# Attention and a swish layer on one core: one laid-down order for whole chunks, and other PSUM banks for the second third of the numerators

## The chip, the cores and the metric

The kernel runs on one core of a Trainium2 chip. The metric is device time in microseconds, the median of several runs. The span of a profile, from its first to its last instruction, is a little shorter than the device time of the same run (283.0 against 284.75 us for the kernel before).

The engines have these short names: PE is TensorE, the matrix engine; DVE is VectorE; ACT is ScalarE; POOL is GpSimd; SP issues most transfers. Each has its own queue of instructions, taken in order. Matmul results go to PSUM, which has eight banks of 512 float32 columns; everything else lies in SBUF.

## The reference

An attention with a kernel in place of the softmax (relu times a cosine and a sine of the position), for 8 batches of 8 heads with 576 positions of 64 values, feeds a two-layer network with a swish between.

```python
def phi(x, c, s):
    r = np.maximum(x, 0.0)
    return np.concatenate([r * c, r * s], axis=-1)
q_p, k_p = phi(q, cos_w, sin_w), phi(k, cos_w, sin_w)
kv  = np.einsum('bhsf,bhsd->bhfd', k_p, v)
z   = np.sum(k_p, axis=2)
num = np.einsum('bhsf,bhfd->bhsd', q_p, kv)
den = np.einsum('bhsf,bhf->bhs', q_p, z)[..., None] + 1e-06
x   = (num / den)          # then rearranged to 4608 tokens of 512
h   = x @ w_in             # 512 -> 2048
g   = h * (1.0 / (1.0 + np.exp(-beta * h)))
out = g @ w_out            # 2048 -> 512
```

## The kernel before

The 4608 tokens are worked in nine chunks of 512 (c = 0 to 8). In the steady state the loop of chunk c does three things: the hidden layer of chunk c, the attention of batch b = c + 1, whose tokens are needed from the next chunk on, and the output layer of chunk c. From chunk 3 on, half of the hidden layer and all of the output layer use a scheme with seven products of half-sized blocks in place of eight. It needs sums of inputs made in advance, and additions on the results.

The names matter, because the order of the work is written down as strings of them:

- `X Y Z V` are four groups of the hidden layer in the seven-product scheme; `X1` to `X7` are the products, `c1X c5X cuX` the copies of partial results, `a2X a3X a7X` the additions, `SaX SbX` the two Silus at the end. `p0` to `p7` are the other eight groups of the hidden layer, plain ones, and `sp0` to `sp7` their Silus on ACT.
- `K` is the matmul of keys and values, `kt` takes it from PSUM; `N0 N1 N2` are the three thirds of the numerators, `x0 x1 x2` divide them (DVE) and turn them by transfers on SP.
- `s01` to `s34` are sums of the hidden values (DVE) for the output layer: the first digit is the quarter, the second the kind.
- `ox1` to `ox7`, and in the new string `oy1` to `oy7`, are the products of the two halves of the output layer.

The parts that the change touches; cuts are marked.

```python
def h_silu(c, jt, bank):                         # sp..., Sa., Sb.: on ACT
    nc.scalar.activation(gs[c, jt // 4][:, jt % 4], ps[:, bank], AF.Silu, scale=beta[:, jt : jt + 1])

def q_tan(b, jp, behind=None):                   # on POOL: q turned, times the tangent
    got = tan_mul(nc.gpsimd, qs_of(b)[:, jp], qts[b % 2][:, jp], 0, NQ)
    # behind: POOL is made to wait for the last sum
# x_rden, x_mul on DVE: den = num's last column + eps; rden = 1/den; xs = num * rden, all from PSUM

def num_all(b, t, bank):                         # a third of the numerators
    for i in range(3):
        for jp in range(2):
            num_mm(b, 3 * t + i, jp, bank, 2 * i + jp)   # to banks bank and bank + 1

# ... the output layer of one half:
def o_fast(c, pr, banks, cols=0):
    b_ps, e_ps, a_ps = (ps[:, k_, 0:HM] for k_ in banks)
    # ...
    def m1():
        prod(b_ps, g_part(0, 0), B11, True, False, 0 < cols)
        nc.scalar.copy(p1, b_ps)
    def m5():
        prod(e_ps, s_part(S1), T1, True, False, 1 < cols)
        nc.scalar.copy(p5, e_ps)
    def m6():
        prod(b_ps, s_part(S2), T2, False, False, 2 < cols)
        nc.scalar.copy(u, b_ps)
    def m2():
        prod(a_ps, g_part(1, 0), B21, True, True, 3 < cols)
    def m7():
        prod(b_ps, s_part(S3), T3, False, False, 4 < cols)
    def m3():
        prod(e_ps, s_part(S4), B22, False, True, 5 < cols)
    def m4():
        prod(b_ps, g_part(1, 1), T4, False, True, 6 < cols)
        # ... copy to o2 on ACT (the very last one half on ACT, half on DVE), store
    def a2():
        nc.vector.tensor_tensor(o1[:, 0:HM], a_ps, p1, op=ALU.add)
    def a7():
        nc.vector.tensor_tensor(o2[:, HM:DM], b_ps, p5, op=ALU.add)
    def a3():
        nc.vector.tensor_tensor(o1[:, HM:DM], e_ps, u, op=ALU.add)
        store(c, pr, o1)

# store: POOL's queue for c < 7, SP's (and for part of the last chunk ACT's) after that

# ... the loop from chunk 2 on:
parts = (6, 0, 4) if c == 2 else (0, 4, 6)       # banks of the three thirds
banks = (2, 3, parts[0]) if c == 2 else (3, 2, parts[0])
x, y = o_fast(c, 0, banks), o_fast(c, 1, (1, banks[1], parts[0]), cols)
# ...
    h_phase(c, b, x, parts)      # in the order of H_ORDER (chunks 7, 8: H_ORDER_END),
                                 # with products 1 5 6 2 7 3 of x at its end
for j in range(4):
    k_piece(b + 1, j)            # relu of the next keys, ACT
x["a7"](); x["a2"](); x["a3"]()
if b + 2 < B:
    att_q(b + 2)                 # relu of q (DVE), turned by a transfer on SP
y["m1"]()
v_half(b + 1, 1, 0, 1, "act")    # v times sine (ACT) and cosine (DVE)
x["m4"]()
v_half(b + 1, 1, 1, 2, "act")
v_half(b + 1, 0, 0, 3)
if c + 1 < NTC:
    x_sums(c + 1)                # four sums of the next chunk's inputs, DVE
y["m5"]()
v_half(b + 1, 1, 2, 3, "act")
y["m6"](); y["m2"](); y["a2"]()
v_half(b + 1, 0, 3, 5)
y["m7"](); y["a7"]()
v_half(b + 1, 0, 5, 7)
y["m3"](); y["a3"]()
v_half(b + 1, 0, 7, 9)
v_half(b + 1, 1, 3, 9, "act")
y["m4"]()
```

Of the kernel before, what the change touches and what calls it, by code (L numbers as in the profile page):

```python
# [13 lines left out]
ALU = mybir.AluOpType  # L14
# [3 lines left out]
NQ = 9  # L18
# [4 lines left out]
def kernel(  # L23
# [14 lines left out]
    nc = tc.nc  # L38

    B, H, S, D = q.shape  # L40
# [461 lines left out]
    def store(c, tt, o_sb, m0=0, m1=DM):  # L502
        for hf in range(2):
            bb, n = divmod((c * TCH + tt * P) // HP + hf, NQ)
            eng = nc.gpsimd if c < 7 else (nc.sync, nc.scalar)[hf] if c == NTC - 1 and tt % 2 else nc.sync
            eng.dma_start(out=out_v[bb, n][:, m0:m1], in_=o_sb[hf * HP : (hf + 1) * HP, m0:m1])  # L506
# [15 lines left out]
    def o_part(c, tt, part, cols=1):  # L522
        o_mm(c, tt, range(4 * part, 4 * part + 4), cols)

    def o_fast(c, pr, banks, cols=0):

        b_ps, e_ps, a_ps = (ps[:, k_, 0:HM] for k_ in banks)
        tok = slice(pr * P, (pr + 1) * P)
        last = c == NTC - 1 and pr == 1

        def prod(dst, left, right, start, stop, pieces=False):
            order = (0, 1, 2, 3, 4, 5, 7, 6) if c + 1 >= B else range(JT // 2)
            for i in order:
                w = HM // 2 if i and pieces else HM
                for m in range(0, HM, w):
                    nc.tensor.matmul(dst[:, m : m + w], lhsT=left(i), rhs=right[:, i, m : m + w],  # L536
                                     start=start and i == 0,
                                     stop=stop and i == order[-1], skip_group_check=True)

        def g_part(r, hf):  # L540
            def at(i):
                jt = 2 * i + r
                return gs[c, jt // 4][:, jt % 4, hf * (TCH // 2) + pr * P : hf * (TCH // 2) + (pr + 1) * P]
            return at

        def s_part(t):
            return lambda i: t[:, i, tok]

        o1 = osb_pool.tile([P, DM], FP32, name="o_sb", tag="o_sb")
        o2 = osb_pool.tile([P, DM], FP32, name="o_sb", tag="o_sb")  # L550
        p1 = part.tile([P, HM], FP32, name="p1", tag="p1")
        p5 = part.tile([P, HM], FP32, name="p5", tag="p5")
        u = part.tile([P, HM], FP32, name="u", tag="u")

        def m1():
            prod(b_ps, g_part(0, 0), B11, True, False, 0 < cols)
            nc.scalar.copy(p1, b_ps)  # L557

        def m5():
            prod(e_ps, s_part(S1), T1, True, False, 1 < cols)  # L560
            nc.scalar.copy(p5, e_ps)

        def m6():
            prod(b_ps, s_part(S2), T2, False, False, 2 < cols)
            nc.scalar.copy(u, b_ps)

        def m2():
            prod(a_ps, g_part(1, 0), B21, True, True, 3 < cols)

        def m7():  # L570
            prod(b_ps, s_part(S3), T3, False, False, 4 < cols)

        def m3():
            prod(e_ps, s_part(S4), B22, False, True, 5 < cols)

        def m4():
            prod(b_ps, g_part(1, 1), T4, False, True, 6 < cols)
            h = HM // 2 if last else HM
            nc.scalar.copy(o2[:, 0:h], b_ps[:, 0:h])
            if last:  # L580
                nc.vector.tensor_copy(o2[:, h:HM], b_ps[:, h:HM])
            store(c, pr + 2, o2, 0, HM if last else DM)

        def a2():
            nc.vector.tensor_tensor(o1[:, 0:HM], a_ps, p1, op=ALU.add)

        def a7():
            nc.vector.tensor_tensor(o2[:, HM:DM], b_ps, p5, op=ALU.add)
            if last:
                store(c, pr + 2, o2, HM, DM)  # L590

        def a3():
            nc.vector.tensor_tensor(o1[:, HM:DM], e_ps, u, op=ALU.add)
            store(c, pr, o1)

        return {n: f for n, f in locals().items() if n[0] in "ma" and n[1:].isdigit()}


    def warm_pe(count, w=512, bank=1):
# [174 lines left out]
    def x_part(b, t, bank):  # L774
        x_div(t, bank)
        x_turn_dma(b, 3 * t, 3 * t + 3)
# [51 lines left out]
    for slot in range(32):  # L828
        if slot < 16:
            h_group(1, slot)  # L830
        else:
            o_part(1, (slot - 16) // 4, slot % 4, 2 if slot > 20 else 1)
        one_unit(slot)

    def k_piece(b, j):
# [3 lines left out]
        if j == 3 and b + 1 < B:  # L839
            load_raw(b + 1, "k")  # L840

    H_ORDER = (
        "X5 X1 Y1 X2 K c5X c1X X6 X3 cuX c1Y p0 kt X7 sp0 Y5 Y6 a3X cuY a7X p1 c5Y sp1 Y3 Y2 a2X X4 SbX "
        "Y7 a3Y a7Y Z1 c1Z a2Y SaX p2 Z5 Z6 sp2 V1 Y4 cuZ s03 p3 c1V Z7 c5Z V6 Z2 SbY SaY Z3 cuV s01 V5 "
        "a7Z a2Z a3Z p4 V7 c5V V2 a7V s02 Z4 sp3 SaZ p5 sp4 a2V V3 SbZ a3V p6 sp5 s13 p7 V4 s21 SaV s11 "
        "sp6 s04 N0 s22 SbV s12 N1 sp7 N2 ox1b x0 s31 s32 s33 s23 ox5b s24 s34 ox6b s14 ox2 ox7 ox3 x1 "
        "x2")
    H_ORDER_END = (
        "X5 X1 p0 c1X Y5 X6 sp0 c5X X2 Y1 a2X cuX c1Y p1 X3 sp1 X7 Y6 p2 a3X cuY SaX a7X Y2 c5Y X4 sp2 "
        "Y7 Y3 Z1 Z2 SbX c1Z p3 a2Y a3Y SaY V1 Z6 Z5 a7Y sp3 c1V cuZ c5Z Y4 p4 s03 Z3 a2Z SbY sp4 V6 Z7 "  # L850
        "V5 a3Z cuV SaZ a7Z p5 V2 c5V Z4 s11 V3 sp5 SbZ a2V a3V V7 SaV a7V p6 V4 s01 p7 s12 sp6 SbV ox1b "
        "s23 s02 s21 s22 sp7 s31 s33 s32 s04 s13 s24 ox2 s14 ox6b s34 ox5b ox7 ox3")
    H_COLS, O_COLS = {4: 6, 6: 4}, {3: 7, 5: 7}

    def h_phase(c, b, x, parts):
        pairs = {n: h_fast(c, k, ((2, 0, 1), (3, 4, 5), (0, 2, 1), (4, 3, 5))[k]) for k, n in enumerate("XYZV")}
        plain = [2, 3, 6, 7, 10, 11, 14, 15]
        sums = None
        for op in (H_ORDER if b < B else H_ORDER_END).split():
            n = int(op[-1]) if op[-1].isdigit() else None  # L860
            if op == "K":
                kv_mm(b, 0, 4)
                kv_mm(b, 1, 4)
            elif op == "kt":
                kv_take((0, 1), 4)
            elif op[0] == "N":
                num_all(b, n, parts[n])
            elif op[0] == "x":
                x_part(b, n, parts[n])
            elif op[0] == "p":  # L870
                h_plain(c, plain[n], 2 if n == 7 and b < B else 6 + n % 2, 2 if n < H_COLS.get(c, 0) else 1)
            elif op[:2] == "sp":
                h_silu(c, plain[n], 2 if n == 7 and b < B else 6 + n % 2)
            elif op[:2] == "ox":
                x["m" + op[2]]()
            elif op[0] == "s":
                sums = g_sum(c, 2 * int(op[1]), 2 * int(op[1]) + 2, n)
            else:
                pair = op[0] if op[0] in pairs else op[-1]
                pairs[pair][op.replace(pair, "")]()  # L880
            if op == "ox2" and b + 1 < B:
                q_tan(b + 1, 0, sums)
                q_tan(b + 1, 1)

    def h_second():
        for slot in range(16):
# [22 lines left out]

    for c in range(2, NTC):  # L910
        b = c + 1
        parts = (6, 0, 4) if c == 2 else (0, 4, 6)
        cols = O_COLS.get(c, 0)
        banks = (2, 3, parts[0]) if c == 2 else (3, 2, parts[0])
        x, y = o_fast(c, 0, banks), o_fast(c, 1, (1, banks[1], parts[0]), cols)
        if c == 2:
            sums = h_second()
            for t, bank in enumerate(parts):
                num_all(b, t, bank)
            q_tan(b + 1, 0, sums)  # L920
            q_tan(b + 1, 1)
            for i, n in enumerate((1, 5, 6, 2, 7, 3)):
                x[f"m{n}"]()
                if i < 3:
                    x_part(b, i, parts[i])
        else:
            h_phase(c, b, x, parts)
        for j in range(4):
            k_piece(b + 1, j)
        x["a7"]()  # L930
        x["a2"]()
        x["a3"]()
        if b + 2 < B:
            att_q(b + 2)
        y["m1"]()
        v_half(b + 1, 1, 0, 1, "act")
        x["m4"]()
        v_half(b + 1, 1, 1, 2, "act")
        v_half(b + 1, 0, 0, 3)
        if c + 1 < NTC:  # L940
            x_sums(c + 1)
        y["m5"]()
        v_half(b + 1, 1, 2, 3, "act")
        y["m6"]()
        y["m2"]()
        y["a2"]()
        v_half(b + 1, 0, 3, 5)
        y["m7"]()
        y["a7"]()
        v_half(b + 1, 0, 5, 7)  # L950
        y["m3"]()
        y["a3"]()
        v_half(b + 1, 0, 7, 9)
        v_half(b + 1, 1, 3, 9, "act")
        y["m4"]()


# [28 lines left out]
```

## Time and profile before

| | |
|---|---|
| device time, median of 3 | 285.44 us (284.34 to 285.46) |
| span of the profiled run | 283.0 us |
| granted TensorE clock | 0.998 |
| first matmul of chunk 3 | 110.45 us into the span |
| last matmuls end | about 278.83 us into the span |

The page gives the busy share of each engine over the whole span; the chain of waits follows the work that ended last back to what released each piece; the windows give busy time between two moments. A busy PE is not PE at its best, since matmuls are pipelined and their ends are modelled. So the prediction works with the spacing from one piece of work to the next rather than with the duration of one instruction.

### The profile page before, as it was taken

What the parts mean: (1) busy time and instruction counts of PE and PEld (TensorE: products, weight loads), DVE (VectorE), ACT (ScalarE), POOL (GpSimd) and SP (SyncE); (2) the same over time, 40 slices, a digit from 0 to 9 for tenths busy, and PEclk for the clock granted to TensorE, in tenths of its full rate; (3) what the DMA queues carried; (4) which work ended last, traced back from release to release, by engine and by line L of the source; (5) the groups of instructions that cost most, each with busy time, mean ns of one, the idle gap of its engine ahead of it and who ended that gap; (6) DMA issues with size and microseconds to landing.
All of it is one profiled execution on the core that took longest, in us unless ns stands there. A gap on an engine that the chain in (4) does not pass through costs nothing.

```text
span 283.0 us, 8903 instructions
## 1 busy us (share of the span) xinstructions
PE 272.0 (96%) x3690; PEld 196.7 (69%) x3690; DVE 217.9 (77%) x547; ACT 179.2 (63%) x356; POOL 71.0 (25%) x89
## 2 busy tenths in 40 slices
PE   8899999999999999999899989999999999999994
PEld 8454455455865588669887877689868866786583
DVE  5989967659999997689868995899579548725742
ACT  5778756872147476877679576967693288339730
POOL 1444000623390084007500552036200220000000
PEclk9999999999999999999999999999999999999999
DMA  7999999999999959984996399315301620041023
GB/s 235 386 390 383 392 387 317 335 236 397 168 261 355 251 123 261 172 318 57 254 279 234 58 258 227 113 35 129 76 2 30 133 74 0 10 102 42 0 59 92
DMA packets 50584, 54.00 MB, mean 191 GB/s; under 512 B 31200, under 2 KB 31472, under 8 KB 50544
## 3 DMA queue, kind: packets, MB, share of 16 engines
q1 hardware_dynamic: 47584, 45.82, 57.2%
q0 software_dynamic: 2688, 7.34, 9.4%
q8 instruction: 29, 0.48, 0.7%
q10 hardware_dynamic: 272, 0.27, 0.3%
q14 instruction: 11, 0.09, 0.1%
HBM read 36.71 MB, written 9.44 MB: 163 GB/s over the span
## 4 chain that ended last, share of the span: by engine, by line
PE 88%; DVE 7%; ACT 2%; issue 1%; ACTq 0%; DVEq 0%
PE ps L536 27%; PE ps L426 15%; PE ps L378 14%; PE ps L465 13%; PE ps L513 10%; PE ps L272 3%; PE ps L293 3%; ACT g_t L417 1%; PE ps L601 1%; DVE qb L194 1%; PE ps L234 1%; DVE S L397 1%; DVE xs L315 1%; DVE vb L219 1%; DVE qs L222 1%
## 5 line engine op out<-in xcount | busy, mean ns | idle before, releaser
L417 ACT ACTIVATE g_t<-ps,beta 128x512 bf16<-128x512 f32 x96 | 62.5, 696 | 7.2 <-PE ps L426 6.0
L426 PE MATMUL ps<-xt,win 128*128 128x512 bf16 (+1 forms) x222 | 48.7, 350 | 0.0
L536 PEld LDWEIGHTS <-S 128*128 128x128 bf16 x504 | 44.7, 98 | 5.2 <-DVE S L397 0.7
L506 POOL DMA_DIRECT2D out_dram<-o_sb x56 | 32.1, 578 | 63.0 <-ACT o_sb L519 24.9
L378 PE MATMUL ps<-xt,win 128*128 128x512 bf16 (+1 forms) x196 | 42.8, 375 | 0.1
L386 ACT ACTIVATE g_t<-ps,beta 128x512 bf16<-128x512 f32 x48 | 32.6, 689 | 10.5 <-PE ps L378 9.9
L536 PEld LDWEIGHTS <-g_t 128*128 128x128 bf16 x378 | 33.1, 98 | 7.4 <-issue 2.2
L378 PEld LDWEIGHTS <-win 128*128 128x128 bf16 x196 | 18.7, 98 | 21.1 <-issue 0.5
L222 POOL TENSOR_TENSOR qs<-qt,tanr 128x1152 bf16<-128x1152 bf16 x8 | 19.0, 2389 | 48.7 <-DVE den L304 33.8
L426 PEld LDWEIGHTS <-win 128*128 128x128 bf16 x222 | 21.7, 98 | 12.5
L536 PE MATMUL ps<-wout,g_t 128*128 128x256 bf16 (+1 forms) x252 | 29.2, 261 | 0.9 <-ACT g_t L417 0.9
L513 PE MATMUL ps<-wout,g_t 128*128 128x512 bf16 (+1 forms) x170 | 29.2, 327 | 0.0
L536 PE MATMUL ps<-T,S 128*128 128x256 bf16 (+1 forms) x252 | 27.2, 261 | 0.2
L536 PE MATMUL ps<-wout,S 128*128 128x256 bf16 (+1 forms) x252 | 26.8, 261 | 0.0
L397 DVE TENSOR_TENSOR S<-g_t 128x512 bf16<-128x512 bf16 (+1 forms) x58 | 22.1, 409 | 4.7 <-ACT g_t L417 4.6
L315 DVE TENSOR_TENSOR xs<-ps,rden 128x768 bf16<-128x768 f32 (+4 forms) x26 | 22.8, 884 | 0.8
L465 PE MATMUL ps<-w_stage 128*128 128x256 bf16 x144 | 23.3, 273 | 0.0
L513 PEld LDWEIGHTS <-g_t 128*128 128x128 bf16 x170 | 16.2, 98 | 9.9
L465 PEld LDWEIGHTS <-w_stage 128*128 128x128 bf16 x192 | 18.4, 98 | 6.7
L219 DVE TENSOR_SCALAR vb<-raw_v,cos 128x256 bf16<-128x256 f32 x63 | 23.0, 423 | 0.0
L217 ACT ACTIVATE vb<-raw_v,sin 128x256 bf16<-128x256 f32 (+1 forms) x50 | 21.7, 497 | 0.7 <-DMA raw_v<-in_v_dram 0.7
L557 ACT COPY p<-ps 128x256 f32<-128x256 f32 x14 | 5.2, 372 | 20.4 <-PE ps L536 18.0
(102 smaller groups left out, 410.9 us busy)
## 6 DMA issues: line engine op xcount, KB each, us to landing
raw_v<-in_v_dram SPq DMA_DIRECT2D x7, 1152.0 KB, 10.1
raw_k<-in_k_dram SPq DMA_DIRECT2D x7, 1152.0 KB, 9.6
raw_q<-in_q_dram SPq DMA_DIRECT2D x7, 1152.0 KB, 7.8
out_dram<-o_sb POOLq DMA_DIRECT2D x56, 128.0 KB, 4.5
w_stage<-in_moe_w_in_dram SPq DMA_DIRECT2D x3, 1024.0 KB, 13.0
w_stage<-in_moe_w_out_dram SPq DMA_DIRECT2D x2, 1024.0 KB, 8.0
w_stage<-in_moe_w_out_dram SPq DMA_DIRECT2D x4, 512.0 KB, 11.9
out_dram<-o_sb SPq DMA_DIRECT2D x13, 128.0 KB, 2.3
```

What stands on the lines that cost most here:

```text
L219: nc.vector.tensor_scalar(o, a, scalar1=t[:, n : n + 1], scalar2=None, op0=ALU.mult)
L222: return eng.tensor_tensor(dst.rearrange("q n (g p) -> q n g p", g=2), src.rearrange("q n (g p) -> q n g p", g=2), tanr[:, n0:n1].unsqueez ...
L315: nc.vector.tensor_tensor(o.rearrange("q j n s d -> q j (n s) d"), nv[:, :, a:z, :, 0:D].rearrange("q j n s d -> q j (n s) d"), rden[:, :, ...
L378: nc.tensor.matmul(ps[:, h_bank(c, jt), blocks.start * 64 : blocks.stop * 64], lhsT=win[jt // 4][:, mi, (jt % 4) * P : (jt % 4 + 1) * P], ...
L386: nc.scalar.activation(gs[c, jt // 4][:, jt % 4], ps[:, h_bank(c, jt)], AF.Silu, scale=beta[:, jt : jt + 1])
L397: return nc.vector.tensor_tensor(o, l, r, op=op)
L417: nc.scalar.activation(gs[c, jt // 4][:, jt % 4], ps[:, bank], AF.Silu, scale=beta[:, jt : jt + 1])
L426: nc.tensor.matmul(ps[:, bank, o * 64 : z * 64], lhsT=win[jt // 4][:, mi, (jt % 4) * P : (jt % 4 + 1) * P], rhs=xt[:, o:z, jp, g * HP : (g ...
L465: nc.tensor.matmul(dst, lhsT=left[:, g], rhs=right[:, :, g * HP : (g + 1) * HP], start=start and g == 0, stop=stop and g == 1, skip_group_ ...
L506: eng.dma_start(out=out_v[bb, n][:, m0:m1], in_=o_sb[hf * HP : (hf + 1) * HP, m0:m1])
L513: nc.tensor.matmul(o_ps[:, m0 : m0 + w], lhsT=gs[c, jt // 4][:, jt % 4, tt * P : (tt + 1) * P], rhs=wout[:, jt, m0 : m0 + w], start=(jt == ...
L536: nc.tensor.matmul(dst[:, m : m + w], lhsT=left(i), rhs=right[:, i, m : m + w], start=start and i == 0, stop=stop and i == order[-1], skip ...
```

## The change

Before, the hidden layer of chunks 3 to 8 had a written order, and the work behind it (output layer, relu of keys and queries, scaling of v, sums of the next chunk's inputs) followed in program code. Now chunks 3 to 8 are one string each, `ORDER` for chunks 3 to 6 and `ORDER_END` for 7 and 8, which holds every operation of the chunk on five queues (PE, DVE, ACT, POOL and SP). For that, each product, copy and addition of the output layer becomes an operation of its own. Its aim is to let each engine find its next piece of work ready, where the code before tied copies and additions to a place behind their products.

New names: `c1o c5o cuo` and `c1y c5y cuy` are copies of the output layer of the first and second half, `c4x c4y` the last copies, `o2x o3x o7x` and `o2y o3y o7y` its additions; `k0` to `k3` the relu of keys (ACT), `q0 q1` that of queries (DVE), `v0` to `v8` v times sine (ACT), `w0` to `w8` v times cosine (DVE), `t1` to `t4` the sums of the next chunk's inputs (DVE), `g0 g1` the two `q_tan` on POOL. A store goes out when both parts of its tile are there. The transfers of the next keys, queries and values are issued when the pieces that read the old ones, and the three divisions, have been laid down.

Second, the second third of the numerators goes to banks 6 and 7, the last third to banks 4 and 5. The places in which matmuls are halved move as well. The code of chunk 2 stays in program order, with small shifts.

```diff
-    H_ORDER = (
-        "X5 X1 Y1 X2 K c5X c1X X6 X3 cuX c1Y p0 kt X7 sp0 Y5 Y6 a3X cuY a7X p1 c5Y sp1 Y3 Y2 a2X X4 SbX "
-        "Y7 a3Y a7Y Z1 c1Z a2Y SaX p2 Z5 Z6 sp2 V1 Y4 cuZ s03 p3 c1V Z7 c5Z V6 Z2 SbY SaY Z3 cuV s01 V5 "
-        "a7Z a2Z a3Z p4 V7 c5V V2 a7V s02 Z4 sp3 SaZ p5 sp4 a2V V3 SbZ a3V p6 sp5 s13 p7 V4 s21 SaV s11 "
-        "sp6 s04 N0 s22 SbV s12 N1 sp7 N2 ox1b x0 s31 s32 s33 s23 ox5b s24 s34 ox6b s14 ox2 ox7 ox3 x1 "
-        "x2")
-    H_ORDER_END = (   # ... cut; its end:
-        "V5 a3Z cuV SaZ a7Z p5 V2 c5V Z4 s11 V3 sp5 SbZ a2V a3V V7 SaV a7V p6 V4 s01 p7 s12 sp6 SbV ox1b "
-        "s23 s02 s21 s22 sp7 s31 s33 s32 s04 s13 s24 ox2 s14 ox6b s34 ox5b ox7 ox3")
-    H_COLS, O_COLS = {4: 6, 6: 4}, {3: 7, 5: 7}
+    ORDER = (
+        "Y1 p0 X1 c1X X5 c1Y K X6 c5X X3 kt X2 p1 cuX Y5 Y6 sp0 X7 a3X a2X sp1 Z1 cuY SaX c5Y Y2 a7X Y3 "
+        "c1Z Y7 X4 SbX a3Y p2 a7Y sp2 a2Y s01 s03 Z6 Y4 SbY cuZ Z5 c5Z s02 V1 Z2 a2Z p3 V5 s04 Z3 c1V "
+        "c5V SaY V6 Z7 sp3 p4 p5 V2 a3Z cuV SaZ a7Z s11 Z4 s13 V7 s12 sp4 s14 a2V sp5 V3 p6 p7 a7V V4 "
+        "a3V SbZ sp6 s21 s22 SaV s23 sp7 N0 s24 ox1 SbV N1 N2 x0 c1o s31 s33 ox2 s32 ox5 oy1 ox6 q0 c5o "
+        "s34 q1 k1 ox3 k3 c1y cuo k0 v0 v1 x1 v2 v3 k2 ox7 o2x w6 x2 g0 o3x oy2 o7x o2y w2 w8 oy6 v4 oy5 "
+        "w7 cuy oy7 w0 ox4 v7 v8 t1 w1 t2 v5 c5y w5 o7y v6 w3 t4 oy3 g1 t3 c4x oy4 w4 c4y o3y")
+    ORDER_END = (     # ... cut; its end:
+        "s01 a3Z sp3 sp4 cuV V2 SaZ a7Z V3 a3V p5 a2V p6 sp5 SaV V7 sp6 Z4 p7 s02 a7V s11 SbZ V4 s12 s14 "
+        "sp7 SbV oy1 ox1 s21 s13 s31 c1y ox2 s22 s32 ox5 c1o ox6 cuo c5o o2x s34 s24 s33 s04 oy2 s23 oy6 "
+        "ox3 o3x cuy ox7 oy5 c5y t3 oy7 t1 o2y o7y oy3 o7x t2 oy4 c4y t4 ox4 o3y c4x")
+    H_COLS, O_COLS = {4: 8, 6: 8}, {3: ("4", "25734"), 5: ("4", "25734")}
 # ... o_fast: one entry for each product, copy and addition
+            "1": lambda: prod(b_ps, g_part(0, 0), B11, True, False, "1" in cols),
+            # ... 5 6 2 7 3 4 alike
+            "c1": lambda: nc.scalar.copy(p1, b_ps),
+            "c5": lambda: nc.scalar.copy(p5, e_ps),
+            "cu": lambda: nc.scalar.copy(u, b_ps),
+            "c4": stored("2c4", c4),
+            "a2": stored("1a2", lambda: nc.vector.tensor_tensor(o1[:, 0:HM], a_ps, p1, **add)),
+            "a3": stored("1a3", lambda: nc.vector.tensor_tensor(o1[:, HM:DM], e_ps, u, **add)),
+            "a7": stored("2a7", lambda: nc.vector.tensor_tensor(o2[:, HM:DM], b_ps, p5, **add)),
 # ... chunk(), in place of h_phase and of what followed it
+            elif op[0] == "g":
+                if b + 1 < B:
+                    q_tan(b + 1, n, None if n else last_sum)
 # ... the loop
-        parts = (6, 0, 4) if c == 2 else (0, 4, 6)
+        parts = (6, 0, 4) if c == 2 else (0, 6, 4)
 # ...
-            h_phase(c, b, x, parts)
-        for j in range(4):
-            k_piece(b + 1, j)
-        # ... down to y["m4"]()
+            chunk(c, b, x, y, parts)
```

## The prediction

> **What bounds the kernel now.** I read the page's busy shares first, then cut the span into chunks, then asked which waits TensorE (PE) has from chunk 3 on. PE is busy in 96% of the span; VectorE (DVE) has the next largest share.
>
> ```profile
> PE 272.0 (96%) x3690; PEld 196.7 (69%) x3690; DVE 217.9 (77%) x547; ACT 179.2 (63%) x356; POOL 71.0 (25%) x89
> ```
>
> So only about 11 us of the span are visibly PE-idle. Next, stretches from the first matmul of one chunk to the first of the next, chunks 3 to 8 (columns: stretch, length, then busy us and count of PE, PE weight load, DVE, ACT, POOL, then clock, DMA share, GB/s):
>
> ```profile
> 110.45:140.00 29.55, 28.41 (x468) 22.54 (x466) 24.62 (x64) 21.32 (x45) 9.19 (x10) 1.00 0.90 205
> 140.00:169.58 29.58, 28.33 (x437) 23.58 (x435) 24.69 (x65) 21.33 (x45) 9.24 (x10) 1.00 0.77 215
> 169.58:198.08 28.50, 28.24 (x467) 22.51 (x466) 23.59 (x63) 21.32 (x45) 8.95 (x11) 1.00 0.56 127
> 198.08:226.49 28.41, 28.15 (x430) 22.99 (x429) 20.20 (x53) 15.37 (x32) 4.12 (x9) 1.00 0.28 60
> 226.49:252.68 26.19, 25.66 (x202) 19.40 (x201) 15.65 (x42) 15.20 (x32) 2.02 (x4) 1.00 0.17 41
> 252.68:278.83 26.15, 25.61 (x201) 19.17 (x198) 14.22 (x38) 15.20 (x32) 0.00 (x0) 1.00 0.18 42
> ```
>
> The reader is to see that chunks doing the same matmuls take 29.6 us early and 28.4 us later, with the clock at 1.00 throughout. What is the floor? From the chain of waits, pieces without a stall: one plain hidden group (4 matmuls of 512 columns) 0.865 us, one fast product of the hidden layer (2 of 256) 0.218, one output product (8 of 256) 0.873, the key-value sums K 1.15, the numerators about 1.2. A chunk 3 to 6 is 8 x 0.865 + 28 x 0.218 + 14 x 0.873 + 1.15 + 1.2 = 27.6 us; chunks 7 and 8, without K and numerators, 25.2 us. Above the floor lie 1.95, 1.98, 0.9, 0.8, 1.0 and 0.9 us, **7.5 us in all**. That is the most that reordering alone can win in these chunks; 110 us ahead of them and 4.2 us behind the last matmul are hardly touched. PE's own waits from 110 us on:
>
> ```profile
> PE ps L536 <- DVE o_sb L588: 1.9, 2, 1.0
> PE ps L293 <- ACT g_t L417: 1.0, 4, 0.3
> PE ps L536 <- ACT g_t L417: 0.9, 2, 0.5
> ```
>
> First line: in chunks 3 and 4 the last output product waits for the addition `a7` of the same half, which sits late in DVE's queue. Second: in each of four chunks the numerators wait for a Silu. Third: in chunks 7 and 8 the first output product waits for a Silu. Pipelined ends hide further pieces, so these 3.8 us are the visible half of the 7.5.
>
> Why is DVE late in chunks 3 and 4? In the output stretch 156.1 to 169.58 it is busy 13.27 of 13.48 us. Part of that is not work. GpSimd (POOL) and DVE:
>
> ```profile
> 159.03 4.74 POOL L222 TENSOR_TENSOR w_stage<-qt,tanr 128x1152 bf16<-128x1152 bf16 x2 [16.91 <-DVE den L304]
> 162.37 2.02 DVE L194 TENSOR_SCALAR qb<-raw_q 128x1152 bf16<-128x1152 f32 x1
> ...
> 64.05 2.92 DVE L406 TENSOR_TENSOR T<-wout 128x1024 bf16<-128x1024 bf16 x1
> ```
>
> The relu of q takes 752 ns by its median; here it takes 2.02 us, over 0.6 us past the end of POOL's second `q_tan`. The sum of weights takes 0.68 us when alone, here 2.92.
>
> **What the Trainium skill says.** "SBUF — State Buffer", section "SBUF: two separate sides": GpSimd and DVE share a port pair as "an exclusive lock, not a bandwidth split", held for the whole instruction; a DVE instruction needs it in a 2-port mode or with two SBUF inputs. The trace agrees: relus of q, scalings of v and SBUF sums stretch until POOL ends, while the divisions of numerators and the output additions, which read PSUM, keep their 0.96 and 0.41 us below it. "VectorE: DVE Perf Modes", section "Why PSUM operands drop a tier", says that PSUM operands exclude that mode; consistent with this. "Perfetto Trace Analysis", section "Identifying the Most-Contended Engine", warns that matmul busy time is a poor measure; agreed, hence the floor from spacings.
>
> **The change part by part.** No arithmetic is added or taken away; the count of PE's instructions is the same, since halved matmuls move between chunks (two halves of a product take 0.87 us like the whole, so nothing from that).
>
> (a) Numerators. Before, the second third goes to banks 4, 5, which need the Silu `SbV`, last but one on ACT. In chunk 4 the numerators begin at about 154.1 and the last Silu ends at 155.63, some 1.4 us later. The change puts the second third in banks 6, 7 (free after `sp6`, in the new string three Silus ahead of `SbV`, which is now the last) and output product 1 (0.87 us) between first and second third. PE gets to the third third 0.4 + 0.87 + 0.4 = 1.67 us after the numerators' start, behind the last Silu. The 0.7 us per chunk that this stretch now loses (0.26 us shown, the rest in pipelined ends) goes in chunks 3 to 6: -2.8 us, if nothing takes it back.
>
> (b) Output stretch of chunks 3 and 4. I lay out DVE from t = 0 at the start of the numerators. Names are those of the order string. Spacings from DVE's rows in the trace: division of a third 1.34, sum 0.335, relu of q 0.67, addition 0.33, scaling of v (`w`) 0.27. x0 ends at 2.0; s31 s33 s32 at 3.0; q0 3.7; s34 4.0; q1 4.7; x1 6.0; o2x 6.3. POOL's first `q_tan` is released by s34 and gets the ports behind q1: 4.75 to 7.15. So w6 waits and ends at 7.4; x2 8.75; o3x 9.1; o7x, o2y 9.75; w2, w8 10.3. **Now the new collision:** POOL's queue is in order: first `q_tan`, two stores released by o3x (0.5 us each, 9.3 to 10.4), second `q_tan`, which waits for nothing else. It runs 10.4 to 12.8, and DVE has nothing but w and t there, all SBUF to SBUF. So w0 ends at 13.1, then t1 w1 t2 w5, and o7y at 14.65. PE meanwhile: ox2 2.1 to 3.0, eight products to ox7 7.3, oy2, oy6, oy5 10.05 (0.1 lost on o3x), oy7, ox4, oy3 12.7; oy4 must wait for o7y: 14.75 instead of 12.7. Loss about 2.1 us, 2.2 with the small one, against 1.95 and 1.98 now: +0.2 us each. In the kernel before both `q_tan` lay back to back under three divisions and additions from PSUM and cost DVE only some 1.3 us.
>
> (c) Chunk 5 has no q: DVE is 1.35 us earlier, second `q_tan` 9.2 to 11.6, o7y 13.5, oy4 0.85 us late. Same as the 0.9 now: 0.
>
> (d) Chunk 6 has no `q_tan` and no v: 0.8 to about 0.1: -0.7.
>
> (e) Chunks 7, 8: two first products (oy1, ox1, 1.75 us) stand ahead of the one that needs the last Silu, and the last Silu ends about 1.9 us after PE comes to the output stretch (chain of waits, chunk 7: Silu from 240.91 for 0.60, output from 239.57). 0.95 and 0.91 to about 0.2: -1.45 together.
>
> (f) End: the last matmuls are now ox4, whose half is copied whole on ACT (0.37) and stored by two 128 KB stores on one queue, where two 64 KB ones went out on two queues: about +0.3.
>
> Sum, with the gain of (a) inside (b) to (d): +0.2 +0.2 +0 -0.7 -1.45 +0.3 = **-1.4 us**, laid on the median of 285.4: 284.0.
>
> **The rivals.** *First: the second `q_tan` costs nothing that PE sees* (its start comes elsewhere, or DVE gets between). Then o7y ends near 12.4, chunks 3 to 5 lose about 0.2 each: -1.75 -1.8 -0.7, and the sum is -6.1, 279.3 us. For it: the order is so close to fitting without the lock that it looks made for that. Against it: two trace cases, one of them scalings of v below `q_tan`, where two of them took 4.3 us. *Second: the first `q_tan` takes the ports ahead of q1.* Then x1 and all behind it slip up to 2.4 us in chunks 3 and 4, bank 0 comes free late for oy2, and both lose another 1 us: 286. Against it: q1 starts at the usual spacing, before s34 has ended. *Third: the hidden stretch stalls in its new order*; by the same layout ACT's Silus and PE stay within 0.3 us, so some tenths at most. *Fourth: transfers.* The transpose of q holds the SP queue 7 to 8 us, but it still starts after x2; hidden.
>
> **Range and chances.** I give the collision three chances in four (284.0) and the first rival one (279.3); the mean is 282.8, and I take 283.0. The range covers both: 279.6 to 285.6. Faster by over 2% is below 279.7, nearly all of the 7.5 us: 0.13. Slower by 2% is above 291: 0.02.
>
> **What would show it.** (a) right: no PE wait at L293 for a Silu. (b) right: in chunks 3, 4 scalings of v of 2 us below the second `q_tan`, then PE waiting 1 to 2 us at oy4 for the addition of a7; chunks 29.6 to 30 us. (d), (e): chunk 6 at 27.7, 7 and 8 at 25.4. Wrong, if chunks 3 to 5 come near 27.8 (first rival), or if q1 takes over 2 us (second).

## The result, and the profile after

The changed kernel takes **288.51 us** (median of 4 runs, 288.1 to 289.11) against 285.40 for the kernel before. The ratio is 1.0119, with a 95% interval of 1.0089 to 1.0149: slower by 1.2%, where 283.0 in a range of 279.6 to 285.6 had been foretold. The spans of the two profiles differ by 3.5 us (286.5 against 283.0), and the account below closes on that.

The page of the changed kernel, busy shares and queue of instruction transfers:

```profile
PE 272.6 (95%) x3690; PEld 198.1 (69%) x3690; DVE 224.9 (78%) x547; ACT 176.4 (62%) x356; POOL 71.5 (25%) x89
...
q8 instruction: 29, 0.48, 0.7%
```

The engines have as many instructions as before; DVE is busy 7 us longer with the same 547. So some of them take longer. The same stretches as before, chunks 3 to 8 of the changed kernel:

```profile
112.08:142.21 30.13, 28.42 (x459) 22.35 (x459) 26.62 (x64) 20.39 (x44) 9.31 (x10) 1.00 0.77 186
142.21:172.38 30.17, 28.38 (x444) 24.08 (x442) 26.73 (x64) 20.76 (x45) 9.32 (x10) 1.00 0.75 204
172.38:201.94 29.56, 28.41 (x460) 22.34 (x458) 25.68 (x63) 20.76 (x45) 9.04 (x10) 1.00 0.60 125
201.94:230.16 28.22, 28.22 (x444) 24.08 (x441) 21.04 (x54) 15.10 (x32) 3.97 (x8) 1.00 0.24 53
230.16:255.41 25.25, 25.25 (x203) 19.58 (x200) 15.61 (x42) 14.92 (x32) 2.21 (x5) 1.00 0.17 43
255.41:281.00 25.59, 25.57 (x202) 19.47 (x199) 14.41 (x39) 14.62 (x32) 0.00 (x0) 1.00 0.21 48
```

The account, from the first matmul of a chunk to that of the next in both traces (before: 110.29, 139.84, 169.41, 197.92, 226.32, 252.52; last output matmul ends at 278.88; by the timeline the first matmul of chunk 3 starts at 110.29, not at 110.45 as the table of before has it):

| piece | before | after | difference | foretold |
|---|---|---|---|---|
| up to chunk 3 | 110.29 | 112.08 | +1.79 | 0 |
| chunk 3 | 29.55 | 30.13 | +0.58 | +0.2 |
| chunk 4 | 29.57 | 30.17 | +0.60 | +0.2 |
| chunk 5 | 28.51 | 29.56 | +1.05 | 0 |
| chunk 6 | 28.40 | 28.22 | -0.18 | -0.7 |
| chunks 7 and 8 | 52.56 | 50.84 | -1.72 | -1.45 |
| after the last matmul | 4.12 | 5.50 | +1.38 | +0.3 |
| sum | 283.0 | 286.5 | +3.50 | -1.45 |

And PE's waits from 105 us on, which answer to the three of before:

```profile
PE ps L536 <- DVE o_sb L588: 4.6, 3, 1.8
PE ps L465 <- DVE o_sb L587: 1.7, 1, 1.7
```

Both kinds of wait for a Silu are gone. The wait for the addition `a7` (L588) is there in three chunks in place of two and longer, and a new one stands at the start of chunk 3 (L587 is the addition `a3`).

**Chunks 3 to 5.** POOL and DVE of the changed kernel in chunk 3, the output stretch:

```profile
130.44 0.76 DVE L194 TENSOR_SCALAR qb<-raw_q 128x1152 bf16<-128x1152 f32 x1
...
135.84 3.90 DVE L219 TENSOR_SCALAR vb<-raw_v,cos 128x256 bf16<-128x256 f32 x4
...
140.86 0.41 DVE L588 TENSOR_TENSOR o_sb<-ps,p 128x256 f32<-128x256 f32 x1
```

```profile
130.76 2.68 POOL L222 TENSOR_TENSOR qs<-qt,tanr 128x1152 bf16<-128x1152 bf16 x1 [16.38 <-DVE S L397]
135.55 1.09 POOL L506 DMA_DIRECT2D out_dram<-o_sb  x2 [2.11 <-DVE o_sb L587]
136.66 2.39 POOL L222 TENSOR_TENSOR qs<-qt,tanr 128x1152 bf16<-128x1152 bf16 x1
```

The order is the one that was laid out: first `q_tan`, two stores, second `q_tan`. The relu of q ahead of it keeps its 0.76 us. Under the second `q_tan`, four scalings of v take 3.90 us, where four took 1.17 us in experiment 2 without it. With the numerators' start (126.45) as zero, `o7y` ends at 14.8 and the last product starts at 14.9; foretold were 14.65 and 14.75.

**The start of chunk 3.** PE and DVE of the changed kernel:

```profile
112.08 0.38 PE L465 MATMUL ps<-xt,win 128*128 128x256 bf16 x2 [1.67 <-DVE o_sb L587]
```

```profile
107.89 0.42 DVE L586 TENSOR_TENSOR o_sb<-ps,p 128x256 f32<-128x256 f32 x1 [1.42 <-ACT vb L217]
...
109.10 0.42 DVE L451 TENSOR_TENSOR w_stage<-xt 128x512 bf16<-128x512 bf16 x1
...
110.56 1.14 DVE L219 TENSOR_SCALAR vb<-raw_v,cos 128x256 bf16<-128x256 f32 x4
111.61 0.42 DVE L587 TENSOR_TENSOR o_sb<-ps,u 128x256 f32<-128x256 f32 x1
```

The "small shifts" in chunk 2 put four sums of inputs and four scalings in front of `a3`, which reads bank 3. They now stand behind the additions `a2` (L586) and `a7`, and DVE is idle for 1.42 us ahead of `a2`. The new string begins with Y1, which writes bank 3. The old one began with X5, which writes bank 0.

**The end.** ScalarE's queue of the changed kernel:

```profile
280.79 1.39 ACTq L506 DMA_DIRECT2D out_dram<-o_sb  x2
282.27 0.37 ACT L557 COPY o_sb<-ps 128x256 f32<-128x256 f32 x1 [1.84 <-issue]
```

The last product ends at 281.0, but the copy of its result starts at 282.27, behind two store issues in the same queue.

### The profile page after: what moved, and what is told of

Its sections match the earlier page's. It is cut to its first block, busy times and chain, and to the rows that moved or that the text cites. A ratio compares the mean times of both kernels' runs of the same rounds, so it can differ in the third digit from the quotient of the medians.

```text
span 286.5 us, 8871 instructions
## 1 busy us (share of the span) xinstructions
PE 272.6 (95%) x3690; PEld 198.1 (69%) x3690; DVE 224.9 (78%) x547; ACT 176.4 (62%) x356; POOL 71.5 (25%) x89
## 4 chain that ended last, share of the span: by engine, by line
PE 77%; DVE 9%; DMA 8%; issue 2%; SPq 1%; ACTq 0%; DVEq 0%; ACT 0%
PE ps L536 24%; PE ps L426 15%; PE ps L465 13%; PE ps L378 12%; PE ps L513 7%; DMA raw_q<-in_q_dram 5%; DVE vb L219 4%; PE ps L293 4%; DMA raw_v<-in_v_dram 3%; PE ps L272 2%; DVE xs L315 1%; SPq L79 1%; DVE w_stage L855 1%; DVE o_sb L586 1%; DVE o_sb L588 0%
## 5 line engine op out<-in xcount | busy, mean ns | idle before, releaser
L417 ACT ACTIVATE g_t<-ps,beta 128x512 bf16<-128x512 f32 x96 | 61.3, 696 | 5.1 <-PE ps L426 5.0
L386 ACT ACTIVATE g_t<-ps,beta 128x512 bf16<-128x512 f32 x48 | 32.6, 688 | 10.5 <-PE ps L378 9.9
L378 PEld LDWEIGHTS <-win 128*128 128x128 bf16 x196 | 18.8, 98 | 21.1 <-issue 0.2
L219 DVE TENSOR_SCALAR vb<-raw_v,cos 128x256 bf16<-128x256 f32 x63 | 32.3, 565 | 0.3 <-DMA raw_v<-in_v_dram 0.3
L426 PEld LDWEIGHTS <-win 128*128 128x128 bf16 x240 | 23.5, 98 | 12.5
L536 PE MATMUL ps<-wout,g_t 128*128 128x256 bf16 (+1 forms) x238 | 28.5, 267 | 0.0
L536 PE MATMUL ps<-T,S 128*128 128x256 bf16 (+1 forms) x238 | 27.8, 267 | 0.0
L536 PE MATMUL ps<-wout,S 128*128 128x256 bf16 (+1 forms) x252 | 27.5, 261 | 0.0
L465 PE MATMUL ps<-w_stage 128*128 128x256 bf16 x144 | 25.6, 273 | 0.0
L536 PE MATMUL ps<-T,g_t 128*128 128x256 bf16 (+1 forms) x140 | 14.3, 251 | 4.6 <-DVE o_sb L588 4.6
```

Of the source, the lines that this page charges most:

```text
L219: nc.vector.tensor_scalar(o, a, scalar1=t[:, n : n + 1], scalar2=None, op0=ALU.mult)
L378: nc.tensor.matmul(ps[:, h_bank(c, jt), blocks.start * 64 : blocks.stop * 64], lhsT=win[jt // 4][:, mi, (jt % 4) * P : (jt % 4 + 1) * P], ...
L386: nc.scalar.activation(gs[c, jt // 4][:, jt % 4], ps[:, h_bank(c, jt)], AF.Silu, scale=beta[:, jt : jt + 1])
L426: nc.tensor.matmul(ps[:, bank, o * 64 : z * 64], lhsT=win[jt // 4][:, mi, (jt % 4) * P : (jt % 4 + 1) * P], rhs=xt[:, o:z, jp, g * HP : (g ...
L465: nc.tensor.matmul(dst, lhsT=left[:, g], rhs=right[:, :, g * HP : (g + 1) * HP], start=start and g == 0, stop=stop and g == 1, skip_group_ ...
```

## Experiments

Each is timed against the kernel before on the same chip, so the ratios to it are compared. Chunk lengths are from one profile each, read as above.

**1. The end of chunk 2 as it was.** The four sums of inputs come before product 5, into the time in which DVE was idle, and two of the four scalings come before product 7. DVE then has two operations between `a7` and `a3` in place of eight (the expectation speaks of three less).

```diff
+            x_sums(c + 1)
             y["5"]()
 # ...
             y["a2"]()
+            v_half(b + 1, 0, 3, 5)
             y["7"]()
             y["a7"]()
-            x_sums(c + 1)
-            v_half(b + 1, 0, 3, 7)
+            v_half(b + 1, 0, 5, 7)
             y["3"]()
```

> The changed kernel with one thing put back: at the end of chunk 2 the four sums of the next chunk's inputs and the scalings of v stand where they stood before the change, so that the addition a3 of the second half has only three operations of VectorE less in front of it. Theory (VectorE's order at the end of chunk 2 holds a bank): the wait of 1.67 us of the first matmul of chunk 3 for that addition goes, and chunk 3 starts near 110.3 us in place of 112.1; time about 286.8. Rival (the wait comes from the new order of chunk 3, which begins with the product that writes that bank where the old one began with another): a wait of over 1 us stays at the same place although the addition comes sooner, and the time stays within 0.5 us of 288.5.

286.33 us, ratio 1.0045 (1.001 to 1.008). Chunk 3 starts at 109.95, the wait for L587 is gone, and chunks 3 to 8 keep their lengths (30.13, 30.19, 29.56, 28.22, 25.24, 25.60). The addition `a3` now starts at 109.35 in place of 111.61. The theory holds: DVE's order at the end of chunk 2 held the bank. The rival falls, though the new first product is what makes the bank urgent.

**2. The second `q_tan` behind the first.**

```diff
-  "... ox7 o2x w6 x2 g0 o3x ...  oy3 g1 t3 c4x ..."
+  "... ox7 o2x w6 x2 g0 g1 o3x ...  oy3 t3 c4x ..."
```

> The changed kernel with one word moved: the second q_tan on GpSimd right behind the first, ahead of the two stores. Theory (GpSimd's second q_tan shuts VectorE out while VectorE has only SBUF-to-SBUF work): it now falls under divisions and additions that read PSUM; scalings of v no longer stretch to over 2 us behind 2.9 us of additions, the wait of TensorE for addition a7 in chunks 3, 4, 5 (1.7, 1.8, 1.15 us) goes, chunks 3, 4 take about 28.2 us in place of 30.1 and chunk 5 about 28.2 in place of 29.6: time about 283.5. Rival (VectorE is late by the sum of its work alone): those waits stay within 0.4 us of what they are and the time stays near 288.5. Second rival (the collision only moves to an earlier place): scaling w6 or a sum stretches to 2.5 us or more ahead of the third division, and half of the gain or less is left, 286 to 287.

284.99 us, ratio 0.9993 (0.9968 to 1.0018). POOL and DVE of this kernel in chunk 3:

```profile
130.75 5.08 POOL L222 TENSOR_TENSOR qs<-qt,tanr 128x1152 bf16<-128x1152 bf16 x2 [16.36 <-DVE S L397]
```

```profile
132.77 0.82 DVE L219 TENSOR_SCALAR vb<-raw_v,cos 128x256 bf16<-128x256 f32 x1
...
135.83 1.17 DVE L219 TENSOR_SCALAR vb<-raw_v,cos 128x256 bf16<-128x256 f32 x4
```

Both `q_tan` now lie under divisions and additions from PSUM. One scaling (w6) still waits between them, 0.82 us; the four behind take 1.17 in place of 3.90. PE's waits for L588 are gone. Chunk 3 takes 28.26 us in place of 30.13, chunk 5 28.27 in place of 29.56. Chunk 4 takes 29.45, with a gap of 1.06 us in the numerators that the profile puts down to "issue"; more of it below. So the collision, not the sum of DVE's work, cost 1.9 us in chunk 3 and 1.3 in chunk 5.

**3. The very last copy on DVE.**

```diff
+            if c == NTC - 1 and pr == 0:
+                nc.vector.tensor_copy(o2[:, 0:HM], b_ps)
+                return
             nc.scalar.copy(o2[:, 0:h], b_ps[:, 0:h])
```

> The changed kernel with the very last copy from PSUM (first half of the output layer of the last chunk) on VectorE in place of ScalarE. Theory (that copy stands in ScalarE's queue behind two store issues of 1.39 us and starts 1.4 us after its matmul's end): the copy starts about 0.4 us after the matmul's end, the time from the last matmul to the span's end falls from 5.66 us to about 4.6, time about 287.4. Rival (the end is set by the stores' own transfer and issue on the SP queue): the end stays within 0.3 us, 288.3 or so.

288.1 us, ratio 1.0127 (1.0062 to 1.0192). From the last matmul's end (280.75) to the span's end (285.8) it now takes 5.05 us in place of 5.5. The copy starts at once:

```profile
278.68 4.24 SPq L506 DMA_DIRECT2D out_dram<-o_sb  x5
...
280.79 0.42 DVE L558 COPY o_sb<-ps 128x256 f32<-128x256 f32 x1
```

But only 0.45 us come of 1.4 us. SP's queue now issues longest, five stores until 282.9. The queue of ACT was one part of the loss. That the stores on one queue are the other is not shown: run 5 spreads the last ones over two queues, and its end is as long. With the time itself no gain can be told.

**4. The bank change alone, in the kernel before.**

```diff
-        parts = (6, 0, 4) if c == 2 else (0, 4, 6)
+        parts = (6, 0, 4) if c == 2 else (0, 6, 4)
```

> The kernel before with the bank change alone: second third of the numerators to banks 6 and 7, last third to 4 and 5, old order. As predicted (0.7 us per chunk of 3 to 6 comes from waits for Silus): the numerators' stretch shrinks and the time falls by 1 to 2.5 us, 283 to 284.4. Theory after the result (most of the 0.7 us is TensorE's own cost of going from 128 by 128 tiles to 64 by 64 and back, and only the shown 0.26 us is a wait; in the old order the last third still needs the Silu that the second third needed): the stretch from the last hidden product to the first output product stays within 0.3 us of 1.87 us, and the time within 0.8 us of 285.4.

284.29 us, ratio 0.9977 (0.9962 to 0.9992). Chunks 5 and 6 shorten from 28.51 and 28.40 to 28.17 and 28.09; chunks 3 and 4 stay at 29.57. PE's waits:

```profile
PE ps L536 <- DVE o_sb L588: 1.4, 2, 1.2
PE ps L293 <- issue: 1.0, 1, 1.0
```

In chunk 3 the wait for `a7` takes back what comes earlier (1.23 us in place of 0.88). In chunk 4 most of that wait is gone, but a gap of 1.04 us stands in the numerators; more of such gaps below. So the Silu wait was worth about 0.3 us per chunk, not 0.7, and the step (a) of the prediction falls by its size. The stretch from the last hidden product to the first output product shrinks from 1.87 to 1.45 us, a little more than the 0.3 us that the theory allowed.

**5. The three repairs together**: 1, 2, and the last strings with product 4 of the first half ahead of that of the second.

```diff
-  "... o7x t2 oy4 c4y t4 ox4 o3y c4x"
+  "... o7x t2 ox4 c4x t4 oy4 c4y o3y"
```

> The changed kernel with three things put right together: the end of chunk 2 in the old order, the second q_tan right behind the first, and in the last strings product 4 of the first output half ahead of product 4 of the second, so that the span ends with a copy in two halves and stores on two queues, as before. If the three losses are independent, their gains add up: 1.8 us at the start of chunk 3, 1.9, 1.9 and 1.3 in chunks 3, 4, 5, and 1.2 at the end, from 288.5 to about 280.5, and 281.5 with the stray PE gap of 1.1 us that one of the runs showed. Rival (the output stretch is bound by VectorE's sum of work, and an earlier chunk 3 only meets it sooner): chunks 3 to 5 lengthen by what chunk 2 gains, 283 or more.

282.66 us, ratio 0.9927 (0.9908 to 0.9947): faster than both kernels. In the profiled run, of 281.21 us, the view of waits lists none for PE from 105 us on. Its chunks 3 to 5:

```profile
110.38:138.65 28.27, 28.27 (x461) 22.32 (x459) 24.36 (x65) 20.76 (x45) 9.09 (x10) 1.00 0.93 204
138.65:166.90 28.25, 28.25 (x444) 24.12 (x442) 23.98 (x63) 20.76 (x45) 9.19 (x11) 1.00 0.83 206
166.90:195.16 28.26, 28.26 (x460) 22.32 (x458) 23.36 (x61) 20.76 (x45) 8.94 (x11) 1.00 0.71 149
```

In the profiles the gains of chunks 2 to 5 add up, and DVE is busy 2.3 to 2.8 us less per chunk. The end takes 5.0 us, still 0.9 above that of before: 0.4 us are won there, where 1.2 had been expected. The last string still has the addition `o3y` behind the last copy, so its stores go out last. The last issue of a store ends 2.1 us after the last matmul in place of 1.4, and the span ends 2.9 us after that in place of 2.7. No run moved `o3y`. The median, too, falls short of the 280.5 to 281.5 us expected: the profiled run is the fastest of 18. The 28.25 us are 0.65 above the floor of 27.6 with no wait left. That is what the next two runs are for.

**6. The last third of the numerators apart**, behind output product 2.

```diff
-  "... SbV N1 N2 x0 c1o s31 s33 ox2 s32 ..."
+  "... SbV N1 x0 c1o s31 s33 ox2 N2 s32 ..."
```

> The kernel with the three repairs, and the last third of the numerators behind output product 2, so that the 64 by 64 tiles stand in three groups between 128 by 128 ones in place of two. Theory (each change between tile shapes costs TensorE some 0.3 us by itself, which is why taking the Silu waits away gave less than the 0.7 us per chunk): chunks 3 to 6 lengthen by 0.2 to 0.4 us each, time up by about 1 us on the kernel with three repairs. Rival (the rest of the 0.7 us was still a wait for Silus): chunks 3 to 6 stay the same or shorten, since this third comes 0.9 us later.

283.34 us, ratio 0.9935 (0.9913 to 0.9958). Chunks 3, 5 and 6 take 28.56, 28.56 and 28.51, that is 0.29 us more than in 5; chunk 4 has a stray gap of 1.10 us. As the theory has it.

**7. The three thirds together**, behind output product 1.

```diff
-  "... sp7 N0 s24 ox1 SbV N1 N2 x0 c1o s31 s33 ox2 s32 ox5 oy1 ..."
+  "... sp7 ox1 s24 SbV N0 N1 N2 s31 x0 c1o s33 ox5 s32 ox2 oy1 ..."
```

> The kernel with the three repairs, and output product 1 ahead of all three thirds of the numerators, which then stand together; product 5 goes ahead of product 2 so that TensorE has work while the first third is divided, and sum s31 ahead of the first division. Theory (changes of tile shape cost some 0.3 us): chunks 3 to 6 shorten by 0.2 to 0.4 us each, about 1 us in all. Rival (Silu waits): the first product now comes sooner than its Silu and TensorE waits at it by 0.3 us or more, nothing gained.

283.32 us, ratio 0.9946 (0.9931 to 0.996). No gain: chunks 5 and 6 take 28.23 and 28.19, chunk 3 28.51, and chunk 4 has a stray gap of 1.96 us. The numerators themselves did shrink. From the last product ahead to the first product behind them they take, in chunk 5, 1.95 us in three groups (6), 1.65 in two (5), 1.46 in one (7). The lines below show it for 5 and 7: from the start of a product, plus its 0.22 us (hidden layer) or 0.87 us (output layer), to the start of the next product, 0.61 + 1.04 us in 5 and 1.46 us in 7.

```profile
180.95 0.38 PE L465 MATMUL ps<-w_stage,win 128*128 128x256 bf16 x2
181.78 1.05 PE L536 MATMUL ps<-wout,g_t 128*128 128x256 bf16 x8
183.69 1.05 PE L536 MATMUL ps<-wout,g_t 128*128 128x256 bf16 x8
```

```profile
183.66 1.04 PE L536 MATMUL ps<-wout,g_t 128*128 128x256 bf16 x8
185.99 1.05 PE L536 MATMUL ps<-T,S 128*128 128x256 bf16 x8
```

But in 7 product 2 then starts 1.05 us after product 5 in place of 0.87, and the 0.2 us are given back. So each further group of 64 by 64 tiles between 128 by 128 ones, a change there and back, costs 0.2 to 0.3 us. The Trainium skill, "TensorEngine Tiling (Array Packing)", section "Key Properties", says that a change of tiling mode drains TensorE. The trace agrees with a cost of that kind; the drain itself is not seen in it.

**8. The three repairs with the old banks.**

```diff
-        parts = (6, 0, 4) if c == 2 else (0, 6, 4)
+        parts = (6, 0, 4) if c == 2 else (0, 4, 6)
```

> The kernel with the three repairs and the old banks (second third of the numerators in 4 and 5, last third in 6 and 7). As predicted (the bank change takes a wait away): a wait for a Silu of 0.2 to 0.6 us comes back at the second third in chunks 3 to 6, 1 to 2 us in all. Theory after the result (with a product between the thirds the Silu is there in time in either order): chunk lengths within 0.2 us of those with the new banks.

282.82 us, ratio 0.9931 (0.9916 to 0.9946). Chunks 3, 5 and 6 take 28.26, 28.27, 28.22, as with the new banks (chunk 4 is left out: in the profiled run it has a gap of 2.90 us in its numerators, and behind it, from 158 to 162 us, the granted clock was 0.50). With a product between the thirds the banks don't matter.

**9 and 10. The halved matmuls.** Runs 2, 4, 6, 7 and 8 showed a stray gap in chunk 4's numerators, put down to "issue": PE stands still and waits for nothing that the profile shows. Two runs change where matmuls are halved: none in chunks 3 to 8, or as the kernel before had them.

```diff
-    H_COLS, O_COLS = {4: 8, 6: 8}, {3: ("4", "25734"), 5: ("4", "25734")}
+    H_COLS, O_COLS = {}, {}                                             # 9
+    H_COLS, O_COLS = {4: 6, 6: 4}, {3: ("", "1562734"), 5: ("", "1562734")}  # 10, and slot > 20
```

> The kernel with the three repairs, and no matmul of chunks 3 to 8 halved (132 matmuls fewer, the same columns). Prediction and theory: two halves take what the whole takes, so every chunk stays within 0.1 us of the kernel with three repairs and its 28.25 us. Rival one (the halves cost): chunks 3 to 6 shorten by 0.2 us or more. Rival two (the halves shift where TensorE's instruction stream falls, and with it the stray gap of 1 to 3 us that some runs show in the numerators of chunk 4): chunk lengths stay, but that gap comes, goes or moves to another chunk.

> The kernel with the three repairs, and the halved matmuls where the kernel before had them (30 more in the hidden layers of chunks 4 and 6, 98 in the second output halves of chunks 3 and 5, four more in chunk 1). Prediction and theory: the moving of halves is neutral, chunks within 0.1 us, time within 0.5 us of the kernel with three repairs (282.7). Rival (the halves stand where they do to keep the stray gap away): a gap of 1 us or more in another chunk than 4, or in every profile, and a time 1 us higher.

9: **280.83 us, ratio 0.9867 (0.9843 to 0.989)**, the best of all. Chunks 3 to 6 take 28.16, 28.16, 28.16, 28.15: halves cost 0.1 us per chunk, and no gap shows. Chunk 3:

```profile
109.87:138.03 28.16, 28.16 (x419) 21.75 (x417) 24.32 (x65) 20.78 (x45) 9.09 (x10) 1.00 0.95 197
```

10: 282.51 us, ratio 0.9901 (0.9875 to 0.9928), with a gap of 1.61 us in chunk 4 and 28.28, 28.29, 28.19 in the others. So where the halves stand is not neutral: less through their own cost than through the gap.

**11 and 12. No halves at all**, also not in chunk 1, with the three repairs and in the kernel before.

```diff
-            o_part(1, (slot - 16) // 4, slot % 4, 2 if slot > 21 else 1)
+            o_part(1, (slot - 16) // 4, slot % 4)
```

> The kernel with the three repairs and no halved matmul anywhere, chunk 1 included. Theory (halves give nothing, and the stray gap in the numerators of chunk 4 was tied to them): chunks 3 to 6 at 28.16 us without a gap, time within 0.5 us of 280.8. Rival (the place of the instruction stream decides, and the run without halves in chunks 3 to 8 was a lucky place): the gap of 1 us or more is back in some chunk, 282 or more.

> The kernel before without any halved matmul. If halves cost the same in every order: chunks 3 to 6 shorten by 0.1 us each and the time falls by 0.3 to 1 us, 284.4 or so. Rival (the kernel before had placed them so that a gap is avoided): a gap of 1 us or more appears and the time rises to 286 or more.

11: 283.66 us, ratio 0.9951 (0.9927 to 0.9975). 12: 287.19 us, ratio 1.0062 (1.0028 to 1.0096). The rivals won. With 76 (11) and 84 (12) instructions of PE fewer in chunk 1 there is a gap of 2.10 us (11) and 1.69 us (12) at the same place, in the output stretch of chunk 2, while chunks 3 to 6 take 28.15 to 28.16 us in 11. Run 9 was indeed a lucky place. PE's timeline of 7 and of 11 at the gap:

```profile
157.71 0.22 PE L293 MATMUL ps<-kv,qt 64*64 64x65 bf16 x3 [1.96 <-issue]
```

```profile
102.96 0.83 PE L536 MATMUL ps<-wout,g_t 128*128 128x256 bf16 x6 [2.10 <-issue]
```

The DMA view of the same two runs, in the 0.2 us from 155.2 and from 100.4:

```profile
q8 instruction: 1, 0.02, 34.2%
```

```profile
q8 instruction: 1, 0.02, 27.9%
```

| run | instruction transfer seen from | gap ends | between |
|---|---|---|---|
| 2 | 155.6 | 158.11 | 2.5 |
| 4 | 154.2 | 156.66 | 2.5 |
| 6 | 155.8 | 158.26 | 2.5 |
| 7 | 155.2 | 157.71 | 2.5 |
| 8 | 155.8 | 158.16 | 2.4 |
| 10 | 153.8 | 156.41 | 2.6 |
| 11 | 100.4 | 102.96 | 2.6 |
| 12 | 100.0 | 102.59 | 2.6 |

In all eight the gap ends 2.4 to 2.6 us after an instruction transfer (read in steps of 0.2 us) of some 16 KB, 0.48 MB by 29; in run 8 it had begun before the transfer. The numerators are 144 matmuls with as many weight loads, 288 instructions in 1.2 us, the densest stretch of the stream. It fits that PE runs out of instructions in or close behind this stretch and goes on when the transfer has brought the next ones. No run changed the transfer alone, so this is argued and not shown, and the place of the transfer doesn't decide it by itself: in 9 one is seen from 181.6, 1.1 us after the start of the numerators of chunk 5, in 11 one from 212.2, 1.0 us after those of chunk 6, and no gap follows. Shown is that the gap moves when the count of instructions ahead of it changes (11, 12). The count alone doesn't decide it either: the profile of 5 has no gap, that of 2, with the same count, has one. As each kernel was profiled once, the profiles don't show whether the gap comes and goes from one execution to the next.

## Why the prediction was wrong

The measured difference lies 4.95 us above the foretold one in the account. Of these, 1.79 us come from the end of chunk 2, a path that the prediction left out; 2.35 from chunks 3 to 6, for the most part because a cost of tile shapes was taken for a wait that the banks would remove; 1.08 from the end of the kernel; chunks 7 and 8 were 0.27 better.

**The bounds (now 7.5 us above the floor).** The floor of 27.6 us was too low by 0.55 us per chunk: without any wait and without halves a chunk takes 28.16. The missing term is for the most part the change of tile shape around the numerators, which I had priced by their matmuls alone. So some 2.2 of the 7.5 us, in chunks 3 to 6, were won by no order tried here; the shortest of these chunks in any run takes 28.09 us (run 4, chunk 6).

**(a) Numerators: mis-sized.** The wait for the Silu went, as foretold. It was worth 0.3 us per chunk (run 4), not 0.7; the rest is the cost of tile shapes, and the new place of product 1 adds one more group of 64 by 64 tiles, about 0.2 us (run 7 against 5). This is why chunk 6 won 0.18 us and not 0.7, and it is most of what is missing in chunks 3 and 4.

**(b) Chunks 3 and 4: the mechanism right, the sum short.** The second `q_tan` did shut DVE out, `o7y` came within 0.2 us of the time laid out, PE waited 1.7 and 1.8 us; run 2 took it away and won 1.9 us in chunk 3. The loss was +0.6 in place of +0.2, through (a).

**(c) Chunk 5: wrong.** Foretold 0, measured +1.05. The wait was 1.15 us in place of 0.85, and I set it against an excess of 0.9 that the order could not win back, since most of it was cost of tile shapes.

**The end of chunk 2: missed.** I called 110 us "hardly touched" and read the small shifts in the diff without laying out DVE there as I did for chunk 3. They cost 1.79 us, half of the whole difference (run 1).

**(e) Chunks 7 and 8: right**, -1.72 against -1.45.

**(f) The end: mis-sized**, +1.38 against +0.3. I priced the copy and the stores, but not that the copy stands behind store issues of 1.39 us in ACT's queue, nor five issues in SP's (run 3), nor that the stores of `o3y` go out behind the last copy (run 5). Run 3 accounts for 0.45 us; no run splits up the rest.

**Rivals.** The first (the second `q_tan` costs nothing) fell by run 2, yet it had pulled my number down by 1.0 us. The second fell too: q1 took 0.76 us. The third and fourth showed no sign. The rival that I lacked was a wait made outside the rewritten chunks.

**The halves: neutral in themselves, not in their effect.** I wrote "nothing from that". They cost 0.1 us per chunk and move a gap of 1 to 2 us (runs 9 to 12). In the two kernels compared the count of instructions is the same, and no such gap was the cause of the 3.5 us.

## What to carry to other kernels

When an order is laid down anew, lay out every queue at the seams too: what ran last before it and holds a bank, and what the last copy stands behind. Keep GpSimd's elementwise work under VectorE work that reads PSUM; its place in the queue, behind stores, decides where it falls. Before calling a distance to the floor winnable, look for the same excess in a chunk without waits.

## What the runs showed of the hardware

Four scalings of v take 1.17 us by themselves and 3.90 us under a `q_tan` on GpSimd. Each further group of 64 by 64 tiles between 128 by 128 ones costs 0.2 to 0.3 us (1.46, 1.65 and 1.95 us for the same numerators in one, two and three groups). With 76 to 84 PE instructions fewer in chunk 1 a gap of 1.7 to 2.1 us stands in the output stretch of chunk 2, and the kernel before is 0.6% slower without halves (run 12); the gaps end 2.4 to 2.6 us after an instruction transfer. Left open: whether that transfer is the cause, and how much of the 0.9 us at the end of run 5 another place of `o3y` would win.
